# Wider column matmuls in block 0, and 64-row tile pairs for gate and up of the last 512 rows

## The chip, the cores and the metric

The kernel runs on one core of one Trainium2 chip. The metric is the device time of one execution in microseconds (us). A core has a matrix engine (TensorE, PE in the profile, with its weight loads listed apart as PEld), a vector engine (VectorE, DVE), a scalar engine (ScalarE, ACT), GpSimd (POOL) and a sync engine (SyncE, SP) whose queue issues nearly all transfers (DMAs). The engines run side by side and wait for one another by semaphores. Matmuls write to PSUM, a buffer of eight banks; this kernel uses it as four tiles of two banks each. Everything else lies in SBUF.

## The reference, cut to what matters

Input and output are 2048 rows (S) of 576 values (D), in bf16. The rows pass a modulated layer norm, a long convolution over the rows, a gate, a second modulated layer norm and a feed-forward block of width 4608 (F):

```python
mod = (silu(c) @ w_mod).reshape(1, 6, 1, 576)      # sa, ca, ga, sb, cb, gb
h = layernorm(x) * (1 + ca) + sa
x = x + ga * A(h, k, v, shift_k, ssm_k, ssm_D)     # h * (causal convolution of kv with ssm_k, + kv * D)
h = layernorm(x) * (1 + cb) + sb
gate = h @ w1                                      # 2048x576 @ 576x4608
up   = h @ w3
x = x + gb * ((silu(gate) * up) @ w2)              # 2048x4608 @ 4608x576
```

The feed-forward block has most of the arithmetic. The change touches two places: how the columns `1 + cb` and `sb` are computed from `c` and `w_mod`, and how `gate` and `up` of the last 512 rows are computed.

## The kernel before, in words

**Blocks.** The convolution works on blocks of 256 rows, numbered 0 to 7. `first_block` (lines 628 to 713) does block 0 alone. Its instructions on DVE, ACT and PE are pinned to the written order by `in_order`. The feed-forward block works on four row blocks of 512 rows, r = 0 to 3 (`row_blocks`, line 1033): for each, `stream` computes the hidden values `h3` (gate, up, SiLU and product), and then `down` multiplies them with `w2`. The steps of the convolution of the next two blocks are woven into `stream` and `down` of r = 0 to 2 by a planner: each piece of feed-forward work adds its cost in us to a due time (`advance`), and steps are emitted until the due time is spent. During r = 3 nothing is left to weave in. Outside of `first_block` the order on each engine comes from the compiler's scheduler, which keeps the written order as a priority and passes over instructions that its model has as not ready.

**The columns of block 0.** The modulation row is needed as columns for the second layer norm, since there the features lie on partitions. `mod_columns` (lines 236 to 251) computes them on PE: for each of the two vectors (`cb`, `sb`) and each of six slices j of 128 or 64 features, five matmuls over the 576 inputs (four with 128 rows and one with 64) with a slice of `w_mod` as the stationary operand and one column of `crep` as the moving one. `crep` (line 202) holds silu(c) repeated in 128 equal columns. The results lie in columns j of a PSUM bank, and ACT copies five of them to `cbcol` and `sbcol` (lines 250 and 251). After it, in order on PE, come: the 16 matmuls of 288 columns of `w_spectrum(1)` (line 299), six matmuls whose result nobody reads (`warm`, line 626), the transposes of the first 128 normalised rows (`turn_split`, line 578), and so on to the first matmuls of the feed-forward block. The transposes also need `h2row` from DVE (line 477).

**Gate and up.** `h2T` holds the normalised rows, transposed, as five slices of the 576 features: four of 128 partitions, and the last 64 features in slice 4, there twice, on partitions 0 to 63 and 64 to 127. One weight tile `wst` holds 512 hidden columns (one group fc of four columns blocks f of 128): slices 0 to 3 for gate, 5 to 8 for up, and slice 4 has the 64 remaining rows of gate on partitions 0 to 63 and those of up on 64 to 127. `load_w13` (line 861) fills it with four DMAs: 512 KB and 64 KB each for `w1` and `w3`. Two such tiles take turns in r = 3. In `stream` one item is one f: `full` (line 916) makes eight matmuls of 128 rows and 512 columns, four for gate and four for up, in two PSUM banks; `rest` (line 927) makes the two matmuls of 64 rows, which lie on different halves of the array and write different banks. For r = 3 the items go in fours: `full` of items 0 and 1, `rest` of items 0 to 3, `hide` of items 0 and 1, then `full` and `hide` of items 2 and 3. `hide` (line 931) is ACT (SiLU of gate, line 934, copy of up, line 936) and DVE (the product, line 938). The order of the SP queue in r = 3 is, for each group, the two 64 KB loads (line 868) and then the two 512 KB loads (line 867); each waits until PE has done with what lies there.

Of the kernel before, what the change touches and what calls it, by code (L numbers as in the profile page):

```python
# [9 lines left out]
BF16 = mybir.dt.bfloat16  # L10
F32 = mybir.dt.float32
I32 = mybir.dt.int32
ALU = mybir.AluOpType
ACT = mybir.ActivationFunctionType

P = 128
# [6 lines left out]
NF = F // P  # L23
RB = 512
NRB = S // RB
FC = 4
# [17 lines left out]
class _Kernel:  # L44
# [27 lines left out]
    def setup(self):  # L72
        nc, const = self.nc, self.const
        nc.scalar.preload_act_table(ACT.Silu)
        self.ident = const.tile([P, P], BF16, name="ident")
        self.npi = const.tile([P, 1], F32, name="npi")
        self.ppi = const.tile([P, 1], F32, name="ppi")
        self.neghalf = const.tile([P, 2], F32, name="neghalf")
        self.shk = const.tile([P, 4, D], BF16, name="shk")
        self.drow = const.tile([9, 64], BF16, name="drow")  # L80
        self.dcol = const.tile([P, 5], BF16, name="dcol")
        self.h3 = const.tile([P, NF, RB], BF16, name="h3")
        self.wm = self.h3[:].rearrange("p a b -> p (a b)")
        self.wst = [const.tile([P, 9, FC * P], BF16, name=f"wst{i}") for i in range(NW13)]
        self.w2m = self.wst[2]
        self.h2T = [const.tile([P, 5, RB], BF16, name=f"h2T{i}") for i in range(2)]
        self.h2row = const.tile([P, 2, 640], BF16, name="h2row")
        self.knat = const.tile([P, 5, B], BF16, name="knat")
        self.Xd = self.dram.tile([NBLK, P, 6 * D], BF16, name="Xd")
        self.Vd = self.dram.tile([NBLK, P, 6 * D], BF16, name="Vd")  # L90
        self.arow = const.tile([P, D], BF16, name="arow")
        self.brow = const.tile([P, D], BF16, name="brow")
        self.cbcol = const.tile([P, 5], F32, name="cbcol")
        self.sbcol = const.tile([P, 5], F32, name="sbcol")
        self.gbrow = const.tile([P, D], BF16, name="gbrow")

        self.Fb = const.tile([P, 5, 2, P], BF16, name="Fb")
        self.Fk = const.tile([P, 3, 2, P], BF16, name="Fk")


        self.arow_i = self.hp.tile([P, 2, P], I32, name="b_row", tag="sg")
        coli = self.small.tile([P, 4], I32, name="b_coli", tag="b_coli", bufs=1)
        self.acol = self.small.tile([P, 4], F32, name="b_col", tag="b_col", bufs=1)
        nc.gpsimd.iota(self.arow_i[:], pattern=[[2, 2], [4, P]], base=1, channel_multiplier=0)
        nc.gpsimd.iota(coli[:, 0:2], pattern=[[2, 2]], base=1, channel_multiplier=4)
        nc.gpsimd.iota(coli[:, 2:4], pattern=[[2, 2]], base=0, channel_multiplier=4)
        nc.vector.tensor_copy(self.acol[:], coli[:])
        nc.vector.memset(self.npi[:], -math.pi)
        nc.vector.memset(self.ppi[:], math.pi)
        nc.vector.memset(self.neghalf[:], -0.5)  # L110
        self.one = self.small.tile([1, P], BF16, name="one", tag="one", bufs=1)
        nc.vector.memset(self.one[:], 1.0)
        nc.vector.memset(self.dcol[:], 0.0)
        self.ang = {}
        self.angles(nc.gpsimd, 0)
        make_identity(nc, self.ident[:])
        nc.gpsimd.memset(self.knat[64:P, 4, :], 0.0)
        nc.gpsimd.memset(self.h2T[0][:, 0, :], 0.0)
# [117 lines left out]
    def mod_columns(self):  # L236

        nc = self.nc
        w5 = self.wm[:, 0:5 * 6 * D].rearrange("p (a d) -> p a d", a=5)
        ps = self.ps()  # L240
        for i, m in enumerate((4, 3)):
            for j in range(6):
                lo = min(P * j, 512)
                n = P if j < 4 else 64
                out = ps[0:n, i, j:j + 1] if j < 5 else ps[64:P, i, 4:5]
                for ct in range(5):
                    k = P if ct < 4 else 64
                    nc.tensor.matmul(out, w5[0:k, ct, m * D + lo:m * D + lo + n],
                                     self.crep[0:k, ct, 0:1], start=(ct == 0), stop=(ct == 4))
        nc.scalar.activation(self.cbcol[:], ps[:, 0, 0:5], ACT.Copy, bias=1.0)  # L250
        nc.scalar.copy(self.sbcol[:], ps[:, 1, 0:5])


    def load_kv(self, s, between=None):
# [626 lines left out]
    def stream(self, r, jobs, rate, size):  # L881
# [65 lines left out]
        for k in range(0, len(items), size):  # L947
# [11 lines left out]
            for m in late:  # L959
                full(m, False)  # L960
                hide(m)

    def down(self, r, rate):
        nc = self.nc
        for h in range(2):

            tail = r == NRB - 1 and h == 1
            accs = [self.ps() for _ in range(4 if tail else 2)]
            acc = [accs[t][:, 0, 0:H] if tail else accs[t // 2][:, t % 2, 0:H] for t in range(4)]
            for f0 in range(0, NF, W2C):  # L970
                w = _ap(self.w2m, (h * NF + f0) // W2C % NW2 * W2C * H, [[H, W2C], [1, H]])
                nc.sync.dma_start(w, self.w2[f0 * P:(f0 + W2C) * P, h * H:(h + 1) * H]
                                  .rearrange("(a p) d -> p a d", p=P))
                last = f0 + W2C == NF
                order = [(f, t) for f in range(W2C) for t in range(4)]
                if last:
                    order = [(f, t) for t in range(4) for f in range(W2C)]
                for f, t in order:
                    nc.tensor.matmul(acc[t],  # L979
                                     self.h3[:, f0 + f, t * P:(t + 1) * P], w[:, f, :],  # L980
                                     start=(f0 + f == 0), stop=(f0 + f == NF - 1))
                if h == 1 and f0 // W2C == 5 and r + 1 < NRB:

                    self.end()
                    self.turn_all(2 * r + 3)
                if (f0 // W2C) % 4 == 3:

                    leave = ((self.keep_v, 3), (self.keep_v, 2), (self.keep_x, 2), (self.keep_x, 3)) if r == 0 else ()
                    for keep, i in leave[2 * h + f0 // (4 * W2C):][0:1]:
                        keep(i)  # L990
                self.advance(rate * W2C * 4 * 0.126)
            for t in range(4):
                s, cc = 2 * r + t // 2, t % 2
                x1 = self.xo[s]
                g = self.lnp.tile([P, H], BF16, name="og", tag="og", bufs=2)
                nc.vector.tensor_mul(g[:], acc[t], self.gbrow[:, h * H:(h + 1) * H])  # L996
                nc.vector.tensor_add(x1[:, cc, h * H:(h + 1) * H], x1[:, cc, h * H:(h + 1) * H], g[:])
                if r == NRB - 1:
                    rows = self.out[B * s:B * (s + 1), h * H:(h + 1) * H].rearrange("(p c) d -> p c d", c=2)
                    nc.sync.dma_start(rows[:, cc, :], x1[:, cc, h * H:(h + 1) * H])  # L1000
                elif h == 1 and cc == 1:
                    nc.sync.dma_start(self.out[B * s:B * (s + 1), :].rearrange("(p c) d -> p c d", c=2),
                                      x1[:])
# [29 lines left out]
    def row_blocks(self, n1):  # L1033
        for r in range(NRB):
            cost = 0
            if r + 1 < NRB:
                s0 = 2 * r + 2

                self.begin(self.conv(s0), FIRST_DUE if r == 0 else 0.0)
                cost = CONV_US[r]  # L1040
            time = 110.0 * 0.85 - (N1 * 1.03 if r == 0 else 0)
            rate = cost / time
            if r == 0:

                jobs = [(fc, 256, 512, None, None) for fc in (n1 - 2, n1 - 1)]

                new = [(n1 + i, 0, RB, b, None) for i, b in enumerate((2, 1, 2))]
                again = [(fc, 256, 512, b, None) for fc, b in enumerate((0, 0, 1, 0))]
                while new or again:
                    jobs += new[0:1] + again[0:1]  # L1050
                    new, again = new[1:], again[1:]
            else:
                spills = {1: (self.keep_x, 1), 2: (self.keep_v, 0), 4: (self.keep_v, 1)} if r == 1 else {}
                jobs = [(fc, 0, RB, (r + fc) % 2, (lambda f, i: lambda: f(i))(*spills[fc]) if fc in spills else None)
                        for fc in range(NF // FC)]
            self.stream(r, jobs, rate, 4 if r == NRB - 1 else 2)
            self.down(r, rate)
            self.end()

# [52 lines left out]
```

## Time and profile before

| | |
|---|---|
| median of 5 runs | 518.87 us (518.47 to 519.67) |
| profiled execution | 517.44 us, of which 515.3 us are the span from the first to the last instruction |
| PE busy | 497.0 us (96%), 3362 matmuls |
| DVE, ACT, POOL busy | 340.9, 294.2, 55.7 us |
| mean granted clock of PE | 0.996 |
| line 248, the one-column matmuls | 60, from 22.3 to 26.0 us |
| lines 916 and 927 with r = 3 | 288 and 72 matmuls, from 404.2 to 476.1 us |
| line 979, `down` of r = 3 | 288 matmuls, from 476.1 to 511.5 us |

The busy time of an engine is the time in which at least one of its instructions is under way. Matmuls are pipelined: one of 512 columns lasts 379 ns from its start to its modelled end, but the next one starts 216 ns after it. So the pace of PE is read from start to start, not from the durations. "PEclk" is the share of its full clock that PE was granted in a stretch. The profile also follows the work that ended last back through time, step by step, to what released each piece; that is called the chain below. A "wait" names the engine and line that ended it; "issue" is idle time for which the profile shows no cause.

### The profile page before, as it was taken

The numbers are of one execution on the slowest core, as the hardware profiler recorded it, in microseconds if no ns is written. First come the engines' busy times: TensorE is split into PE (matmuls) and PEld (weight loads), VectorE is DVE, ScalarE is ACT, GpSimd is POOL, SyncE is SP. The second block draws the span as 40 slices with busy tenths as digits, with TensorE's granted clock in tenths as the row PEclk, the third lists the DMA queues.
The fourth block names the chain that finished last, engine by engine and source line by source line (L and its number), as shares of the span: only waits on it lengthen the run. The fifth ranks groups of instructions, "written<-read, shape, count | busy, mean of one in ns | idle before, by whom it ended". The sixth has DMA issues, their size and how long they took to land.

```text
span 515.3 us, 8723 instructions
## 1 busy us (share of the span) xinstructions
PE 497.0 (96%) x3362; PEld 293.7 (57%) x3362; DVE 340.9 (66%) x515; ACT 294.2 (57%) x581; POOL 55.7 (11%) x109
## 2 busy tenths in 40 slices
PE   7999989998999999999999899999999999999997
PEld 3667764556787444344787443434688544444775
DVE  8898899999993364997999984299660212112012
ACT  7668689577443569658553365976816345545000
POOL 3303003104040001203010000120101000000000
PEclk9989999999999999999999999999999999999999
DMA  8957949688979857558999763545455454450462
GB/s 278 316 157 232 296 163 295 190 259 264 297 240 340 259 176 242 172 168 281 354 344 363 269 196 121 198 148 176 141 139 142 144 175 132 153 170 6 119 180 70
DMA packets 102205, 107.77 MB, mean 209 GB/s; under 512 B 5075, under 2 KB 94228, under 8 KB 102164
## 3 DMA queue, kind: packets, MB, share of 16 engines
q1 hardware_dynamic: 102142, 107.21, 65.7%
q8 instruction: 26, 0.43, 0.3%
q14 instruction: 15, 0.12, 0.1%
q10 hardware_dynamic: 22, 0.01, 0.0%
HBM read 96.00 MB, written 11.21 MB: 208 GB/s over the span
## 4 chain that ended last, share of the span: by engine, by line
PE 65%; DVE 20%; ACT 6%; DMA 5%; issue 2%; SPq 1%; DVEq 0%; ACTq 0%
PE ps L916 36%; PE ps L979 18%; PE ps L927 5%; DVE p L410 4%; DVE z L412 3%; DMA wst<-in_B_w_dram 2%; PE ps L313 2%; DMA X<-Xd 2%; PE ps L539 1%; DVE h L938 1%; DVE z L405 1%; DVE kvt L334 1%; ACT junk L440 1%; DVE kv L335 1%; ACT sg L934 1%
## 5 line engine op out<-in xcount | busy, mean ns | idle before, releaser
L916 PE MATMUL ps<-h2T,wst 128*128 128x512 bf16 (+1 forms) x1344 | 264.9, 349 | 2.4 <-ACT h2T L601 1.6
L916 PEld LDWEIGHTS <-wst 128*128 128x128 bf16 x1344 | 127.7, 98 | 122.9 <-issue 19.8
L934 ACT ACTIVATE sg<-ps 128x512 bf16<-128x512 f32 x144 | 86.8, 603 | 112.3 <-PE ps L927 67.5
L979 PE MATMUL ps<-wst,h 128*128 128x288 bf16 x1152 | 145.5, 286 | 3.2 <-ACT u L936 2.2
L979 PEld LDWEIGHTS <-h 128*128 128x128 bf16 x1152 | 112.4, 98 | 32.9 <-issue 4.2
L938 DVE TENSOR_TENSOR h<-sg,u 128x512 bf16<-128x512 bf16 x144 | 60.7, 425 | 96.4 <-ACT u L936 96.3
L936 ACT CAST u<-ps 128x512 bf16<-128x512 f32 x144 | 84.8, 589 | 0.2 <-DVE h L938 0.2
L410 DVE TENSOR_TENSOR p<-X,V 128x3456 bf16<-128x3456 bf16 x28 | 54.8, 1958 | 5.3 <-DMA X<-Xd 5.1
L412 DVE TENSOR_TENSOR z<-z,p 128x3456 bf16<-128x3456 bf16 x28 | 54.8, 1958 | 0.2
L996 DVE TENSOR_TENSOR og<-ps,gbrow 128x288 bf16<-128x288 f32 x32 | 13.2, 453 | 48.8 <-PE ps L979 48.8
L927 PE MATMUL ps<-h2T,wst 64*128 64x512 bf16 (+1 forms) x336 | 42.4, 349 | 0.0
L440 ACT ACTIVATE junk<-x 128x576 bf16<-128x576 bf16 x54 | 37.7, 698 | 0.5
L601 ACT ACTIVATE h2T<-ps,sbcol,cbcol 128x256 bf16<-128x256 bf16 x35 | 16.8, 571 | 24.1 <-PE ps L571 24.1
L927 PEld LDWEIGHTS <-wst 64*128 64x128 bf16 x336 | 11.3, 94 | 27.2 <-issue 24.4
L455 POOL TENSOR_SCALAR l2m<-l2s 128x2 f32<-128x2 f32 x6 | 8.7, 1444 | 153.0 <-ACT junk L440 153.0
L566 ACT ACTIVATE h2row<-x,l2n,l2r 128x576 bf16<-128x576 bf16 (+1 forms) x24 | 13.8, 646 | 12.5 <-POOL l2n L460 12.5
L334 DVE TENSOR_TENSOR kvt<-kh,shk 128x1152 bf16<-128x1152 bf16 x24 | 18.1, 756 | 3.3 <-DMA kh<-in_A_k_dram 3.2
L335 DVE TENSOR_TENSOR kv<-kv,kvt 128x1152 bf16<-128x1152 bf16 x24 | 18.1, 756 | 0.3
L455 POOL TENSOR_SCALAR l1m<-l1s 128x2 f32<-128x2 f32 x7 | 3.0, 423 | 141.3 <-ACT junk L440 141.3
L315 ACT CAST X<-ps 128x576 bf16<-128x576 f32 x24 | 15.5, 657 | 0.0
L405 DVE TENSOR_TENSOR z<-X,V 128x3456 bf16<-128x3456 bf16 x7 | 13.7, 1956 | 2.3 <-DMA X<-Xd 2.3
L745 ACT CAST y<-ps 128x576 bf16<-128x576 f32 x14 | 8.4, 653 | 10.5 <-PE ps L539 10.5
(137 smaller groups left out, 362.1 us busy)
## 6 DMA issues: line engine op xcount, KB each, us to landing
wst<-in_B_w_dram SPq DMA_DIRECT2D x80, 512.0 KB, 4.7
wst<-in_B_w_dram SPq DMA_DIRECT2D x72, 288.0 KB, 3.5
X<-Xd SPq DMA_DIRECT2D x8, 864.0 KB, 5.8
Xd<-X SPq DMA_DIRECT2D x6, 864.0 KB, 5.4
wst<-in_B_w_dram SPq DMA_DIRECT2D x80, 64.0 KB, 2.9
kh<-in_A_k_dram SPq DMA_DIRECT2D x7, 720.0 KB, 8.2
Vd<-V SPq DMA_DIRECT2D x4, 864.0 KB
V<-Vd SPq DMA_DIRECT2D x4, 864.0 KB
```

Source lines behind the costliest of these rows:

```text
L334: nc.vector.tensor_mul(tmp[:], kh[:, 3 - j:5 - j, :], tap(j))
L335: nc.vector.tensor_add(kv[:], kv[:], tmp[:])
L405: nc.vector.tensor_mul(self.accs[s][:], X[:], V[:])
L410: nc.vector.tensor_mul(p[:], X[:], V[:])
L412: nc.vector.tensor_add(z[:], z[:], p[:])
L440: self.nc.scalar.activation(junk[:], src[:, i, :], func, accum_out=out[:, col:col + 1])
L916: nc.tensor.matmul(gus[k][:, i, a * n:(a + 1) * n], w[:, 5 * i + ct, (fi + a) * P:(fi + a + 1) * P], hT[:, ct, t0:t1], start=(first and ct ...
L927: nc.tensor.matmul(gus[k][:, i, a * n:(a + 1) * n], w[rows, 4, (fi + a) * P:(fi + a + 1) * P], hT[rows, 4, t0:t1], start=(first and a == 0 ...
L934: nc.scalar.activation(sg[:], gus[k][:, 0, :], ACT.Silu)
L936: nc.scalar.copy(u[:], gus[k][:, 1, :])
L938: nc.vector.tensor_mul(self.h3[:, f:f + m, t0:t1], sg[:].rearrange("p (a t) -> p a t", a=m), u[:].rearrange("p (a t) -> p a t", a=m))
L979: nc.tensor.matmul(acc[t], self.h3[:, f0 + f, t * P:(t + 1) * P], w[:, f, :], start=(f0 + f == 0), stop=(f0 + f == NF - 1))
```

## The change

In `mod_columns` each matmul takes 100 columns of `crep` in place of one, and so writes 100 equal columns; ACT then reads every hundredth. For r = 3 `stream` is replaced by `stream_halves`. There every matmul of gate and up is one of 64 rows. They come in pairs, one on partitions 0 to 63 and one on 64 to 127 of the same slice. Pass 0 of an f (`part(f, 0)`) gives gate the lower halves and up the upper halves, in five pairs, the fifth being slice 4. Pass 1 (`part(f, 1)`) swaps the two in four pairs: up gets the lower halves and gate the upper ones. So in each pair the two matmuls write different banks, and a bank is written from both halves of the array one after the other. So that pass 1 of an f does not begin before pass 0 is done, GpSimd writes one word (`tok`) after the last matmul of pass 0, and the first matmul of pass 1 waits for that word. Between pass 0 and pass 1 of f lie pass 1 of f-1 and pass 0 of f+1. The loads of the weights stand at the same place in the program, at the first f of a group.

```diff
+        self.tok = const.tile([1, 1], F32, name="tok")
...
-                out = ps[0:n, i, j:j + 1] if j < 5 else ps[64:P, i, 4:5]
+                out = ps[0:n, i, 100 * j:100 * (j + 1)] if j < 5 else ps[64:P, i, 400:500]
...
-                                     self.crep[0:k, ct, 0:1], start=(ct == 0), stop=(ct == 4))
-        nc.scalar.activation(self.cbcol[:], ps[:, 0, 0:5], ACT.Copy, bias=1.0)
-        nc.scalar.copy(self.sbcol[:], ps[:, 1, 0:5])
+                                     self.crep[0:k, ct, 0:100], start=(ct == 0), stop=(ct == 4))
+        nc.scalar.activation(self.cbcol[:], ps[:, 0, 0:500:100], ACT.Copy, bias=1.0)
+        nc.scalar.copy(self.sbcol[:], ps[:, 1, 0:500:100])
...
+    def wait_for(self, later, first):
+
+        self.tc.add_manual_dep(
+            later, first.name,
+            mybir.DependencyInfo(mybir.DependencyClass.Sync, mybir.DependencyReason.DATA),
+            reason="both halves of the rows write this bank, one after the other")
+
+    def stream_halves(self, r):
+
+        nc = self.nc
+        hT = self.h2T[r % 2]
+        newest = lambda: nc.cur_bb.bb.instructions[-1]
+        gus, ws, marks = {}, {}, {}
+
+        def part(f, swap):
+            w = ws[f // FC]
+            cols = slice(f % FC * P, (f % FC + 1) * P)
+            for ct in range(4 if swap else 5):
+                for rows, i in ((slice(0, 64), swap), (slice(64, P), 1 - swap)):
+                    nc.tensor.matmul(gus[f][:, i, :], w[rows, 5 * i + ct if ct < 4 else 4, cols], hT[rows, ct, :],
+                                     start=swap == 0 and ct == 0, stop=swap == 1 and ct == 3)
+                    if swap == 1 and ct == 0 and i == 1:
+                        self.wait_for(newest(), marks.pop(f))
+            if swap == 0:
+                first = newest()
+                nc.gpsimd.memset(self.tok[:], 0.0)
+                marks[f] = newest()
+                self.wait_for(marks[f], first)
+
+        def hide(f):
...
+        for f in range(NF + 1):
+            if f < NF:
+                if f % FC == 0:
+                    self.load_w13(f // FC, (r + f // FC) % 2)
+                    ws[f // FC] = self.w13.pop(f // FC)
+                gus[f] = self.ps()
+                part(f, 0)
+            if f > 0:
+                part(f - 1, 1)
+                hide(f - 1)
...
-            self.stream(r, jobs, rate, 4 if r == NRB - 1 else 2)
+            if r == NRB - 1:
+                self.stream_halves(r)
+            else:
+                self.stream(r, jobs, rate, 2)
```

`hide` inside `stream_halves` is the same three instructions as before, for one f.

## Prediction

> **What bounds the kernel now.** I read the page's totals and chain first: PE is busy for 497.0 of 515.3 us and has 65% of the chain, so PE time saved late in the kernel is time saved. Next comes the chain in order of time around the last row block (start, us, what):
>
> ```profile
> 398.50 5.88 PE ps L979 x48
> 404.38 3.45 PE ps L916 x16
> 407.83 0.97 PE ps L927 x8
> 408.80 7.01 PE ps L916 x32
> 415.81 0.97 PE ps L927 x8
> ...
> 471.70 0.97 PE ps L927 x8
> 472.67 3.56 PE ps L916 x16
> 476.23 33.86 PE ps L979 x276
> ```
>
> From 398 us to 510 us it is PE alone. ACT is busy for 36.8 us and DVE for 16.6 of these 71.9 us of gate and up, POOL for nothing. A group of 32 full matmuls and 8 of 64 rows takes 7.01 + 0.97 = 7.98 us. The waits of the weight loads in this stretch say what is not pure work:
>
> ```profile
> PEld L916 <- issue: 3.8, 9, 0.4
> PEld L927 <- issue: 3.8, 9, 0.4
> ```
>
> Nine times per direction the weight loads stand still for 0.4 us, at each change between 128-row and 64-row matmuls. In the timeline, start to start, full matmuls follow each other after 215.7 ns; the change to 64 rows takes 312 ns (407.452 to 407.764) and the change back 308 ns (408.425 to 408.733). In between the four pairs start at 407.764, 407.990, 408.206 and 408.422: after 226 ns for the first, then 216 ns per pair, the second of a pair 3 ns after the first. A pair so costs what one full matmul costs.
>
> For the other place I read stretches of 3.4 us (us, PE busy, granted clock, DMA share, GB/s), and the timeline:
>
> ```profile
> 22.66:26.07 3.41, 3.41 (x56) 1.00 1.02 373
> 26.07:29.49 3.42, 3.42 (x16) 0.50 1.10 328
> 29.49:32.90 3.41, 3.41 (x24) 1.00 0.71 213
> ```
> ```profile
> 22.31 3.72 PE L248 MATMUL ps<-crep,h 128*128 128x1 bf16 x60
> ...
> 29.44 0.63 DVE L477 TENSOR_SCALAR h2row<-x,l2mv,l2r 128x576 bf16<-128x576 bf16 x2
> ...
> 29.61 1.46 PE L626 MATMUL ps<-shk,ident 128*128 128x512 bf16 x6
> ...
> 30.90 0.44 PE L578 MATMUL ps<-ident,h2row 128*128 128x128 bf16 x5
> ```
>
> While the one-column matmuls run PE looks busy, but streams next to nothing: 56 columns in 3.41 us. At the end of that stretch the clock drops to half, for just one stretch, in which line 299's matmuls start every 240 ns. PE reaches the transposes at 30.90, when their input from DVE (29.44 + 0.63 = 30.07) has long been there.
>
> **What the Trainium skill says.** "TensorE: Matmul & The Clock Gate", Part 1: the clock follows activity in free-running windows of about 3.4 us and is halved after an idle one. The trace agrees: 3.413 us at 0.50. In Part 3 the same page has matmuls on different row groups run together, some 4 ns apart; here 3 ns. "TensorEngine Tiling (Array Packing)", Key Properties, says that a change of tiling mode drains the engine; the trace shows 96 and 92 ns over the usual spacing. The same page, Gotcha 1, says that different row tiles may not use one PSUM bank at the same time, which is why the change swaps banks and orders the passes; no run here shows the contrary.
>
> **The change, part by part.** *Pairs.* Before, the stage runs from 404.215 to 476.064 us: 71.85 us. Its work is 36 f of nine slots (eight full matmuls and one pair), 324 x 0.2157 = 69.89 us; the rest, 1.96 us, is nine groups with 0.217 each, which is 96 + 92 ns for the changes and some 10 ns for the first matmul after each. After, it is 36 x (5 + 4) = 324 pairs, again 69.89 us, and one change in and one out, 0.22 us: 70.11 us. Saved: 1.74 us. It adds 288 matmuls with their weight loads, four instructions per 216 ns; line 248's loads and matmuls start every 25 ns, so issuing them is covered.
>
> *The GpSimd word.* 36 memsets, and a wait on PE's first matmul of each second pass, with all of PE queued behind it, and ACT's `hide` behind PE. The trace has no such memset in this stretch. From the last start of the first pass: 379 ns to its end, about 80 ns to POOL (the usual gap between its dependent operations here), about 100 to 310 ns for a memset (the four 128x1 ones took 99 to 102 ns, line 117's 312), 40 ns back to PE (a matmul at 32.891 began 41 ns after its release): 0.6 to 0.8 us. The cover is pass 1 of f-1 and pass 0 of f+1, nine pairs or 1.94 us; for the first f only five (1.08 us), for the last only four (0.86 us). Both count from the end of a pair's 216 ns slot, so they hold too. Cost from nothing to a few tenths at the two ends; I take nothing. Without the cover it would be 0.6 to 0.8 us x 36, over 20 us.
>
> *Weight loads.* No DMA is added, but their window shrinks: a tile comes free at the end of pass 1 of its last f, which now runs after pass 0 of the next group's first f. The next use is three f later, 3 x 1.94 = 5.83 us, less 0.16 for the last matmul's end, 5.67 us (7.8 before). Both large loads are now wanted at once. Before:
>
> ```profile
> 411.53 1.26 SPq L867 DMA_DIRECT2D wst<-in_B_w_dram  x2
> ```
>
> Issued from 411.53, their last packet ended at 416.05, 4.5 us later, with the second issue 0.86 us after the first. Issued back to back they need about as long or less. With 1.1 us to spare I take nothing. The 64 KB loads come free 2.8 us earlier, with pass 0. If they stood between the large ones in the queue, they would cost some 0.5 us each, still inside.
>
> *Columns.* Line 248 sets 60 matmuls in 3.65 us: about 25 to 39 ns apart within a slice, 96 and 106 ns at the changes to and from 64 rows. At 100 columns a matmul streams for 100/512 of 213 ns, 41.7 ns, and follows after some 44. Within a slice of 128 the starts then lie 55, 44 and 44 ns apart against 39, 25 and 25, 54 ns more, and each of the two changes waits about 40 ns longer: 134 ns per slice of 128, about 107 where slices are 64 wide. 8 x 134 + 4 x 107 = 1.5 us later. The gain stands against it: if the clock holds, line 299 takes 16 x 122.5 ns (line 979's spacing for 288 columns) = 1.96 us, not 3.64. The six fillers would end, and the transposes start, at 27.47 + 1.96 + 1.29 = 30.72 in place of 30.90: 0.18 us earlier. Does the clock hold? The window would now stream for 5 x 41.7 ns in about 425, 49%. Summing the columns of the recorded matmuls, I find windows of 48% (67.0 to 70.5) and 53% (125 to 128.5) with no drop, and the one that dropped at 4%. So it most likely holds. The bounds: 1.15 us later at the transposes, if it drops at 26.07 all the same (line 248 ends at 28.15, line 299 at 30.76, fillers 32.05). Where the window lies otherwise, so that the clock of before never fell, before could start the transposes at 30.13, and after is 0.6 us later. ACT's strided copies have five columns as before; `cbcol` is wanted only at 31.33, which covers their later start.
>
> **Sum.** Against the profiled execution: 517.44 - 1.74 - 0.18 = 515.5 us. The median lies 1.43 us higher; taken from it, 518.87 - 1.92 = 516.95, so 517.0 us. The 1.74 are at the end of the chain and carry over whole. The 0.18 at 33 us may be lost on the way, since DVE and DMAs share the chain between 33 and 290 us. The scheduler also sees longer matmuls in block 0 and may shift a few instructions later on; I allow 1 us either way.
>
> **Rivals.** *The first block takes back most of it.* Either clock case: -1.74 + 1.15 = -0.6, or -1.74 + 0.6 = -1.1, some 518.1 us; with shifts from the scheduler that is no change (0.2% is 1.04 us, about the spread of the runs before, and less can't be told from nothing). For it: the window is free-running, so the drop may not be in every execution. Against: the profiled execution has it.
>
> *Pairs do not hold 216 ns over a long stretch: slower.* Place: the 324 pairs. At 5.4 ns more per pair the gain is gone, from 8.6 ns on the kernel is over 0.2% slower; at 15 ns, the distance of the next weight loads in a burst (407.760 to 407.775), it is +4.9 - 1.7 = +3.1 us, 522 us. The order of the pairs is the scheduler's: if it puts lower and upper halves apart where it believes a load to be late, an f's first pass takes 5 x 0.216 = 1.08 us more. For it: no stretch before has over four pairs. Against: three spacings in a row of 216 ns, with the loads of the third and fourth pair already made during the pair before.
>
> *Nothing gained from the tiles* because the weights come late: if the large loads took 6.7 us and not 4.5, each of seven groups would wait about 1 us, +5 us in sum, 524 us. Against: no other large transfer runs then (DMA share 0.41).
>
> **Numbers.** Forecast as above 0.62 (own range 516.0 to 517.8); first block gives back 0.22 (517.2 to 519.6); pairs or their order 0.11 and late weights 0.05, both over 520. Faster by over 0.2% comes from 0.6 of the first and a little of the second: 0.65; same 0.19; slower 0.16. The range 515.8 to 519.7 leaves out the two slow cases and a few in a hundred below.
>
> **What would show it.** Right: lines of the new matmuls start every 216 ns in pairs, from about 404 to 474 us, no "issue" waits of weight loads inside, no PE wait on POOL, clock 1.00 at 26 to 29.5 us, line 248 about 5.2 us long. Wrong: waits of PE on POOL or on DMA wst every fourth f, halves that run singly, a clock of 0.50 after line 248, or another middle part between 33 and 404 us.

## The result: slower by 0.22%

Over all runs the change takes 519.45 us against 518.28 us before, a ratio of 1.0022 (95% interval 1.0014 to 1.0029), or 1.17 us more. The forecast was 517.0 us, faster. The profiled execution takes 519.67 us, its span 517.4 us against 515.3 us. Lines have moved: line n of the kernel before is n + 1 after in the middle part, 248 is 249, 299 is 300, 405 is 406. The new pairs are line 983, their words line 989, and `down` is line 1026.

The chain around the last row block (start, us, what):

```profile
401.42 5.88 PE ps L1026 x48
407.30 32.76 PE ps L983 x303
440.06 5.78 DMA wst<-in_B_w_dram
445.84 0.05 issue
445.88 32.12 PE ps L983 x296
478.00 33.96 PE ps L1026 x276
```

It is one stretch of pairs now, but for one transfer of weights in the middle. The stage starts 3 us later than before (407.23, before 404.22) and runs to 477.93: 70.70 us, before 71.85. So it gives 1.15 us back, and what these two executions lose lies ahead of it. The waits of this stretch:

```profile
POOL tok L989 <- PE ps L983: 77.1, 36, 12.3
...
PEld L983 <- DMA wst<-in_B_w_dram: 1.3, 2, 1.0
PE ps L983 <- DMA wst<-in_B_w_dram: 0.5, 1, 0.5
...
PEld L983 <- issue: 0.2, 1, 0.2
```

POOL waits for PE, as it should; no wait of PE on POOL is listed. The nine stops per direction at changes between 128 and 64 rows are gone. From start to start the pairs keep 216 ns all through; the longest exception is 869 ns at 445.0.

In block 0, the same three stretches (us, PE busy, clock, DMA share, GB/s) and PE's timeline:

```profile
22.66:26.07 3.41, 3.41 (x44) 1.00 1.02 360
26.07:29.49 3.42, 3.42 (x35) 1.00 1.10 340
29.49:32.90 3.41, 3.41 (x26) 1.00 0.83 236
```
```profile
22.71 5.31 PE L249 MATMUL ps<-crep,h 128*128 128x100 bf16 x60
27.96 2.13 PE L300 MATMUL ps<-kT,Fk 128*128 128x288 bf16 x16
...
31.22 0.44 PE L579 MATMUL ps<-ident,h2row 128*128 128x128 bf16 x5
```

The clock holds. From the first column matmul to the first transpose PE takes 8.51 us (22.71 to 31.22), before 8.59 (22.31 to 30.90). The forecast was 0.18 us earlier; it is 0.08, and this is not where the time went either.

Where it went is seen on DVE, some ten microseconds later. Before:

```profile
39.85 0.76 DVE L335 TENSOR_TENSOR kv<-kv,kvt 128x1152 bf16<-128x1152 bf16 x1
40.52 0.42 DVE L938 TENSOR_TENSOR h<-sg,u 128x512 bf16<-128x512 bf16 x1
40.85 0.75 DVE L337 TENSOR_TENSOR kv<-kv,vt 128x1152 bf16<-128x1152 bf16 x1
41.52 1.95 DVE L405 TENSOR_TENSOR z<-X,V 128x3456 bf16<-128x3456 bf16 x1
```

After:

```profile
39.99 1.96 DVE L406 TENSOR_TENSOR z<-X,V 128x3456 bf16<-128x3456 bf16 x1
41.86 0.43 DVE L939 TENSOR_TENSOR h<-sg,u 128x512 bf16<-128x512 bf16 x1
42.19 0.76 DVE L336 TENSOR_TENSOR kv<-kv,kvt 128x1152 bf16<-128x1152 bf16 x1
42.93 0.42 DVE L939 TENSOR_TENSOR h<-sg,u 128x512 bf16<-128x512 bf16 x1
43.28 0.75 DVE L338 TENSOR_TENSOR kv<-kv,vt 128x1152 bf16<-128x1152 bf16 x1
```

The order has changed: the long product z of block 1 now stands ahead of the last two steps of `kv`. PE needs `kv` for the spectrum of block 1; it does not need z yet. PE's first matmuls of that spectrum, before and then after:

```profile
41.76 2.12 PE L299 MATMUL ps<-kv,Fb 128*128 128x288 bf16 x16
```
```profile
44.17 1.02 PE L300 MATMUL ps<-kv,Fb 128*128 128x288 bf16 x7 [2.10 <-DVE kv L338]
```

Before, PE comes to them with no wait noted; after, it stands idle for 2.10 us until line 338 is done. Counted from the first matmul of gate and up (32.89 and 33.20), the spectrum starts after 8.86 us before and after 10.97 us now. The programs show the same: outside the new stage, SP's order is the same in both, POOL differs by the 36 words and PE by the width of 60 matmuls, but DVE's order differs in a few places between its 70th and its 90th instruction, and ACT's in one swap. How far the delay is carried on can be read from the first matmul of gate and up to the first one of the last row block. In the three profiled kernels with z ahead of the end of `kv` (the change and two of the experiments below) this takes 373.83 to 375.45 us; in the nine others 371.32 to 373.49 us.

### The profile page after: what moved, and what is told of

Its sections match the earlier page's. It is cut to its first block, busy times and chain, and to the rows that moved or that the text cites. A ratio compares the mean times of both kernels' runs of the same rounds, so it can differ in the third digit from the quotient of the medians.

```text
span 517.4 us, 9370 instructions
## 1 busy us (share of the span) xinstructions
PE 496.7 (96%) x3650; PEld 294.5 (57%) x3650; DVE 341.1 (66%) x515; ACT 293.9 (57%) x581; POOL 59.6 (12%) x145
## 4 chain that ended last, share of the span: by engine, by line
PE 69%; DVE 16%; ACT 6%; DMA 4%; issue 2%; POOL 1%; SPq 1%; POOLq 0%; ACTq 0%; DVEq 0%
PE ps L917 26%; PE ps L1026 19%; PE ps L983 13%; PE ps L928 4%; DVE p L411 4%; DMA wst<-in_B_w_dram 4%; DVE z L413 3%; ACT junk L441 2%; PE ps L314 2%; PE ps L540 2%; PE ps L300 1%; PE ps L220 1%; DVE h L939 1%; DVE kvt L335 1%; DVE kv L336 1%
## 5 line engine op out<-in xcount | busy, mean ns | idle before, releaser
L917 PE MATMUL ps<-h2T,wst 128*128 128x512 bf16 (+1 forms) x1056 | 201.0, 341 | 2.3 <-ACT h2T L602 1.6
L917 PEld LDWEIGHTS <-wst 128*128 128x128 bf16 x1056 | 100.2, 98 | 87.3 <-issue 15.5
L939 DVE TENSOR_TENSOR h<-sg,u 128x512 bf16<-128x512 bf16 x108 | 45.4, 424 | 39.3 <-ACT u L937 39.2
L983 PE MATMUL ps<-h2T,wst 64*128 64x512 bf16 x648 | 70.3, 376 | 0.5 <-DMA wst<-in_B_w_dram 0.5
L983 PEld LDWEIGHTS <-wst 64*128 64x128 bf16 x648 | 31.3, 94 | 39.2 <-DMA wst<-in_B_w_dram 1.3
L928 PE MATMUL ps<-h2T,wst 64*128 64x512 bf16 (+1 forms) x264 | 33.3, 342 | 0.9 <-ACT X L316 0.9
L456 POOL TENSOR_SCALAR l1m<-l1s 128x2 f32<-128x2 f32 x7 | 5.6, 806 | 141.7 <-ACT junk L441 141.7
L928 PEld LDWEIGHTS <-wst 64*128 64x128 bf16 x264 | 8.6, 94 | 22.4 <-issue 21.6
```

The costliest lines, as they stand in the source:

```text
L917: nc.tensor.matmul(gus[k][:, i, a * n:(a + 1) * n], w[:, 5 * i + ct, (fi + a) * P:(fi + a + 1) * P], hT[:, ct, t0:t1], start=(first and ct ...
L928: nc.tensor.matmul(gus[k][:, i, a * n:(a + 1) * n], w[rows, 4, (fi + a) * P:(fi + a + 1) * P], hT[rows, 4, t0:t1], start=(first and a == 0 ...
L939: nc.vector.tensor_mul(self.h3[:, f:f + m, t0:t1], sg[:].rearrange("p (a t) -> p a t", a=m), u[:].rearrange("p (a t) -> p a t", a=m))
L983: nc.tensor.matmul(gus[f][:, i, :], w[rows, 5 * i + ct if ct < 4 else 4, cols], hT[rows, ct, :], start=swap == 0 and ct == 0, stop=swap == ...
```

## Experiments

Theory O: the order on DVE costs. Theory W: the work of the longer matmuls costs. Theory H: the pairs of half tiles are slow. All ratios are to the kernel before, with runs on the same chip, 95% interval in brackets.

**100 columns alone.**

```diff
-                out = ps[0:n, i, j:j + 1] if j < 5 else ps[64:P, i, 4:5]
+                out = ps[0:n, i, 100 * j:100 * j + 100] if j < 5 else ps[64:P, i, 400:500]
...
-                                     self.crep[0:k, ct, 0:1], start=(ct == 0), stop=(ct == 4))
+                                     self.crep[0:k, ct, 0:100], start=(ct == 0), stop=(ct == 4))
...
```

> The 100-column matmuls alone, the last row block as before. Theory O (order): with 100 columns the compiler's scheduler orders DVE differently after block 0, the 1.96 us product z at line 405 ahead of the last steps of kv, and that is what costs: 2.3 to 2.9 us slower than before, with line 299's matmuls of x_spectrum(1) starting about 2.4 us later. Theory W (work): the longer matmuls themselves cost, 1.6 us at most where the clock would have held anyway, less otherwise: 0 to 1.6 us slower. Theory H (halves): the tile pairs are what is slow, and this kernel is within 0.5 us of before.

520.01 us, 1.0031 (1.0017 to 1.0044): 1.4 us slower by the medians. The spectrum starts 10.96 us after the first matmul of gate and up, again behind a wait for `kv`:

```profile
43.62 1.79 PE L299 MATMUL ps<-kv,Fb 128*128 128x288 bf16 x7 [2.09 <-DVE kv L337]
```

In this execution PE was busy for only 1.33 of the 3.42 us around the wait, and the clock was 0.50 in the next 3.41 us, a second cost (us, PE busy, clock, DMA share, GB/s). The profiled execution of the change does not have that.

```profile
40.29:43.71 3.42, 1.33 (x13) 1.00 0.97 279
43.71:47.12 3.41, 3.41 (x16) 0.50 0.96 293
```

H is out as the cause of the loss. O expected more than this, W's upper end fits the time, so it takes the next ones to tell.

**The pairs alone.** One column, and the new stage. Of the change's edit this much stays, with the new functions:

```diff
-            self.stream(r, jobs, rate, 4 if r == NRB - 1 else 2)
+            if r == NRB - 1:
+                self.stream_halves(r)
+            else:
+                self.stream(r, jobs, rate, 2)
```

> The 64-row pairs alone, block 0 with one column as before, so DVE's order outside the last row block is that of before. O and W: 1.1 to 1.7 us faster than before (the stage of gate and up in 70.1 to 70.8 us in place of 71.85). H: no faster, or slower by 1 us, with the stage as long as before or longer.

518.05 us, 0.9991 (0.9975 to 1.0008): half a microsecond faster by the medians, and not told from no change. The stage takes 70.56 us, inside what was expected. The 1.3 us that it saves would be 0.9975, at the edge of the interval, so whether they all arrive is not told; the last experiment has a part of the answer.

**Both parts with 80 columns.** At 80 the order on DVE is that of before.

```diff
-                out = ps[0:n, i, 100 * j:100 * (j + 1)] if j < 5 else ps[64:P, i, 400:500]
+                out = ps[0:n, i, 100 * j:100 * j + 80] if j < 5 else ps[64:P, i, 400:480]
...
-                                     self.crep[0:k, ct, 0:100], start=(ct == 0), stop=(ct == 4))
+                                     self.crep[0:k, ct, 0:80], start=(ct == 0), stop=(ct == 4))
```

> Both parts, with 80 columns in place of 100. At 80 the DVE order is that of before. O: 1.0 to 1.9 us faster than before. W: 80% of the cost of 100 columns stays, so about 0.3 us slower to 0.5 us faster than before. H: 1 us slower.

517.70 us, 0.9992 (0.9969 to 1.0015). The interval is too wide to decide between O and W by itself.

**Both parts with 100 columns, z held behind kv.** Only the order on DVE differs from the change.

```diff
         nc.vector.tensor_mul(kv[:], kv[:], vt[:])
+        self.kv_last = nc.cur_bb.bb.instructions[-1]
...
-        yield from self.pair(self.X[0], self.V[1], 1)
+        first = self.pair(self.X[0], self.V[1], 1)
+        with self.tc.issue_after(self.kv_last):
+            c = next(first)
+        yield c
+        yield from first
```

> Both parts with 100 columns, and the product z of block 1 (line 405) made to issue after the last step of kv on DVE. DVE's order is then that of before but for two V steps. O: 1.0 to 1.9 us faster than before, about 2.5 us faster than the change. W: like the change, about 1.2 us slower than before. H: the same, 1 us slower.

517.79 us, 0.9980 (0.9964 to 0.9997), faster than before where the change is slower. W expected 1.2 us slower and falls. The spectrum of block 1 no longer waits:

```profile
41.64 2.12 PE L300 MATMUL ps<-kv,Fb 128*128 128x288 bf16 x16
```

It starts 8.81 us after the first matmul of gate and up. Of all kernels run this is the only one whose interval lies below 1, and only just; the same kernel with its instructions moved, below, has 0.9988 (0.9968 to 1.0008). Neither loses; that the pinned change is faster is not certain.

**The order alone.** The kernel before, one column, no pairs; z written ahead of the last step of `kv` (in the change it stands ahead of the last two).

```diff
-        yield from self.kv_rows(1)
+        rows = self.kv_rows(1)
+        for _ in range(3):
+            yield next(rows)
         yield from self.v_block(1)
         yield from self.pair(self.X[0], self.V[1], 1)
+        yield from rows
```

> The kernel before with one column and without tile pairs; only DVE's order is that of the change: the product z of block 1 issues ahead of the last multiply of kv. O (order): 1.3 to 2.4 us slower than before, line 299's matmuls of x_spectrum(1) starting 1.5 to 2.5 us later. W (the longer matmuls are the cost): no difference, within 0.4 us of before.

520.15 us, 1.0035 (1.0018 to 1.0053), 1.3 us slower by the medians, without one longer matmul. DVE and PE show the same picture as with the change:

```profile
40.95 1.95 DVE L405 TENSOR_TENSOR z<-X,V 128x3456 bf16<-128x3456 bf16 x1
42.82 0.41 DVE L941 TENSOR_TENSOR h<-sg,u 128x512 bf16<-128x512 bf16 x1
43.16 0.75 DVE L337 TENSOR_TENSOR kv<-kv,vt 128x1152 bf16<-128x1152 bf16 x1
```
```profile
44.05 1.14 PE L299 MATMUL ps<-kv,Fb 128*128 128x288 bf16 x8 [2.17 <-DVE kv L337]
```

**80 columns alone.** The matmuls of the third experiment in the kernel before.

> 80 columns alone, with DVE's order of before. O: between 0.3 us faster and 0.7 us slower than before, since what PE spends longer (about 1.2 us) is taken from fillers and from the wait for DVE. W: about 1.3 us slower, four fifths of what 100 columns alone cost.

518.05 us, 0.9987 (0.9970 to 1.0004), by the medians 0.8 us faster, a little more than O expected. The 60 matmuls take 4.59 us from first to last start (3.54 with one column, 5.08 with 100), and no loss follows. W falls here too.

**100 columns alone, z held behind kv.** The edits of the first and the fourth experiment together. O expected to be within 0.6 us of before, W 1.4 us slower.

> 100 columns alone, with the product z of block 1 issued after the last step of kv; no tile pairs. O (order): within 0.6 us of before, so 1.3 to 2.3 us faster than 100 columns with the scheduler's own order; line 299's matmuls of x_spectrum(1) start 8.8 us after the first matmul of gate and up, as before, not 11.0. W (work of the longer matmuls): 1.4 us slower than before, like 100 columns alone.

518.13 us, 0.9999 (0.9985 to 1.0014). The first matmul of gate and up starts at 32.65 us, the spectrum 8.81 us after it and without a wait:

```profile
41.47 2.12 PE L299 MATMUL ps<-kv,Fb 128*128 128x288 bf16 x16
```

The same 60 matmuls cost 0.31% or nothing, according to DVE's order. O is shown from both sides: the order without the columns costs, the columns without the order don't. Why the scheduler's order tips between 80 and 100 columns no run shows.

**Is the slow issue of a load due to instructions being fetched?** Theory F: a load of weights that is issued slowly meets a fetch of instructions, and moving the instructions frees it. In the change, SP's timeline has such a load:

```profile
436.79 1.11 SPq L869 DMA_DIRECT2D wst<-in_B_w_dram  x2
439.59 2.20 SPq L868 DMA_DIRECT2D wst<-in_B_w_dram  x2
444.56 1.12 SPq L869 DMA_DIRECT2D wst<-in_B_w_dram  x2
448.03 0.93 SPq L868 DMA_DIRECT2D wst<-in_B_w_dram  x2
```

The pair of large loads takes 2.20 us to issue at 439.59 and 0.93 at 448.03. The second one began to issue at 440.06, and among the DMA packets the same moment has one of 16 KB on the queue that fetches instructions (1.31 us long). PE then waits 0.65 us beyond its usual spacing. The pairs alone, both parts with 80 columns, and the held version have the slow issue at the same load too (1.28 to 1.42 us), with 0.3, 0 and 0.7 us of PE's time. So the held version and the pairs alone were run again with PE's instructions moved on by 56, in place of four fillers that nobody reads:

```diff
-        self.warm(6, busy)
+        self.warm(2, busy, 32)
...
+        for _ in range(narrow):
+            self.nc.tensor.matmul(ps[:, 0, 0:1], self.ident[:], src[:, 0:1], start=True, stop=True)
```

> Both parts with 100 columns and DVE's order of before, and four of the six unread fillers of block 0 (512 columns each) are made 32 fillers of one column, so that PE's instruction stream is 56 instructions ahead in the last row block. Theory F (fetch): the one slow issue on the SP queue there (1.3 to 1.7 us in place of 0.46) comes from meeting a 16 KB fetch of instructions at the same time; moved by about 3 us it is gone, no matmul waits for weights, and the stage of gate and up takes 70.1 us; 1.7 us faster than before. Against F: the slow issue stays at the same load, with a stall of 0.5 to 0.7 us, stage 70.7.

> The tile pairs alone with one column, with the same 32 short fillers. F: stage of gate and up in 70.1 us, 1.7 us faster than before. Against F: 70.7 us and 0.5 to 1.1 us faster. Set against the kernel with 100 columns and the same order, it says what the columns themselves are worth: nothing to 0.6 us in favour of one column.

In the first of them, the same load:

```profile
436.10 1.11 SPq L876 DMA_DIRECT2D wst<-in_B_w_dram  x2
438.90 0.92 SPq L875 DMA_DIRECT2D wst<-in_B_w_dram  x2
```

The slow issue is gone and the stages take 70.24 and 70.15 us, which speaks for F. The times do not follow: 518.08 us, 0.9988 (0.9968 to 1.0008), and 518.64 us, 0.9997 (0.9982 to 1.0013), not the 1.7 us that were expected. The second is no clean test: its narrow fillers came on top of the one-column matmuls, the clock was 0.50 for 6.83 us from 25.19, and gate and up began 11.51 us after the first column matmul.

The held version with moved instructions has other slow issues instead, of 2.0 and 1.8 us at 252 and 256 us, where the change has none over 0.8. The second of them meets a 16 KB fetch, the first meets none. In the change's own last row block two more fetches, at 413.07 and 428.32, overlap issues of small loads that take their usual 0.47 and 0.48 us. Counted over all twelve traces, after the first 30 us: of 215 issues that overlap a 16 KB fetch 35 take over 1 us, of 3266 that overlap none 42 do; of 24 that begin within 0.1 us of the start of a fetch 14 do. So slow issues are much more frequent beside a fetch, most of all at its start, but a fetch is neither enough nor needed. F stays likely for the one place, and what it is worth in the whole kernel is open.

**The words alone.** Theory T: the words make the end of the program longer. Every kernel with pairs takes 39.5 us from the first matmul of the last `down` to the end of the program; those without take 39.2. The kernel before, with 36 words that no matmul waits for:

```diff
+            if r == NRB - 1:
+                newest = nc.cur_bb.bb.instructions[-1]
+                nc.gpsimd.memset(self.tok[:], 0.0)
+                self.tc.add_manual_dep(
+                    nc.cur_bb.bb.instructions[-1], newest.name,
+                    mybir.DependencyInfo(mybir.DependencyClass.Sync, mybir.DependencyReason.DATA),
+                    reason="word")
```

> The kernel before with the 36 GpSimd words of the last row block and nothing else; no matmul waits for them. Theory T (tail): the 0.3 us more between the first matmul of the last down and the end of the program, which every kernel with tile pairs shows (39.5 us against 39.2), comes from the words: 39.5 us here, 0.3 us slower than before. Rival (tail of the pairs): it comes from the change of the array's mode on entering down: 39.2 us here, and no difference.

The tail is 39.50 us, and the kernel takes 519.69 us, 1.0017 (1.0001 to 1.0034). T holds for the tail. Its rival, that the change from 64 to 128 rows on entering `down` makes it longer, falls, since this kernel enters `down` from 128 rows. The whole time agrees with 0.3 us, but its interval is too wide to measure that. In the profiles the 0.3 us are the very last step: POOL's last instruction starts 0.37 us after the one before it, without words 0.07 us; why, no run shows. A word itself takes 88 ns, as its group in this kernel shows (busy us, mean ns of one, then the idle time before and what ended it):

```profile
L936 POOL MEMSET tok<- 1x1 f32 x36 | 3.2, 88 | 79.9 <-PE ps L928 50.5 <-PE ps L917 22.2 <-DVE h L946 7.3
```

## Why the prediction was wrong, by its own steps

**Sum.** By the profiles the change gives up 2.11 us to DVE's order (10.97 - 8.86), gains 1.15 us in the stage (71.85 - 70.70) and loses 0.29 us at the end: +1.25 us, where the medians differ by 1.17. That these two agree so well is luck in part, since the profiled spans differ by 2.16 us. The rest is 0.40 us ahead of the first column matmul, where no instruction has another order or width, 0.09 us gained from there to gate and up, and 0.60 us between the spectrum and the last row block. That last stretch alone runs from 362.46 us (the kernel before) to 364.63 us over the twelve profiles. By whole times the order costs 1.3 us (alone, by the medians) to 2.2 us (the change against the held version, by the ratios 1.0022 and 0.9980).

**The step that failed** is the sentence that the scheduler "may shift a few instructions later on; I allow 1 us either way". It put at nothing, with a margin for chance, what one mechanism makes 2.11 us in the profile. At 100 columns the scheduler puts a 1.96 us product ahead of the steps that PE waits for; at 80 it doesn't. The place could be seen before: in the trace of the kernel before, DVE's last step of `kv` and z stand right behind each other at 41 us, and PE's spectrum, at 41.76, starts 0.16 us after that step ends. DVE was at that time the engine to look at, and the prediction asked only how much later PE comes out of block 0. That the order would tip at 100 columns could not be read from that trace, but from the order of the program after. The first rival, that block 0 takes most of the gain back, looked near the right place for the wrong mechanism, and ended at "no change"; neither slow rival happened. It is luck that 519.45 us lies within the stated 515.8 to 519.7 us: the term that brought it there was put at nothing. The baseline was off as well: 518.87 us was the median of 5 runs, 518.28 is that of 79.

**Pairs.** The pace was right: 216 ns per pair over 648 matmuls, one change in and one out. The stage was sized at 70.11 us and measured at 70.08 (80 columns) to 70.75 us (held version); the difference is the late weights. The cover of the word was right: no wait of PE on POOL. That the words cost nothing was wrong by 0.3 us, at the end of the program, where nothing hides it.

**Weight loads.** "With 1.1 us to spare I take nothing" took the 4.5 us of one pair of large loads for all. In the change the pair issued from 439.59 landed only at 445.84, 6.25 us later, with one issue of 1.74 us in it, and that reached PE, 0.65 us once. The mechanism of the rival of late weights exists, but at a tenth of its price.

**Columns.** The 60 matmuls were forecast 1.5 us longer and are 1.54 longer (5.08 against 3.54 from first to last start), with starts 54, 44 and 44 ns apart within a slice as worked out. (The 213 ns for 512 columns in that sum follow from two spacings of the trace: (215.7 - 122.5) / (512 - 288) is 0.416 ns per column.) The clock holds; the window over them streamed for 59%, forecast 49%. The gain of 0.18 us at the transposes measured 0.08. The doubt about the baseline was justified: in the pairs alone, with one column, the windows lay otherwise and no drop came,

```profile
21.83:25.24 3.41, 3.41 (x51) 1.00 1.11 332
25.24:28.66 3.42, 3.42 (x47) 1.00 1.04 365
```

and its first matmul of gate and up started 9.26 us after the first column matmul, before 10.58, held version 10.49. In the words alone, with one column too, the drop lasted twice as long and that distance was 11.67 us:

```profile
24.71:28.12 3.41, 3.41 (x33) 0.50 1.08 354
28.12:31.54 3.42, 3.20 (x13) 0.50 0.99 299
```

So the wider matmuls spare a drop that does not come in every execution. Against these distances they gain up to 1.2 us or lose up to 1.2; the loss, for which the prediction had 0.6, is an estimate, since in the pairs alone the columns began 1.3 us later than before (23.59) and DVE, not PE, had the chain there. With 100 columns the distance is 10.43 to 10.49 us in all five profiles. Over many runs no difference is seen (0.9987 with 80 columns, 0.9999 with 100).

The prediction had one window that dropped, at 4%, and two that did not, at 48 and 53%. The twelve profiles narrow this down. Take windows of 3.41 us in line with the recorded drops, from 10 to 505 us, and estimate the streaming by 0.416 ns per column: the ten windows at full clock that a drop followed streamed for 4 to 34% of their time, and no other window at full clock streamed for less than 40%. A few matmuls are missing from some traces.

**What stays open** is how much of the stage's gain arrives. The held version has 0.9980 against 0.9999 for the same columns without pairs: about 1 us. The pairs alone have 0.9991 (0.9975 to 1.0008). But with 80 columns the kernel with pairs has 0.9992 and the one without 0.9987, so there nothing is gained, though its stage is the shortest of all. Less 0.3 for the end, 0.8 to 1.5 us would be expected, and the intervals hold that, but they hold zero too. The slow issues elsewhere may take a part.

## What to carry to other kernels

Where a scheduler orders the instructions, a longer instruction early in the program changes more than its own time: compare the order of every engine before and after, and look at engines that the edit does not touch. Where an engine is shared between work that somebody waits for and work that nobody waits for yet, pin the order there; here one dependency took the same change from 1.0022 to 0.9980 (0.9964 to 0.9997). Count an edit that makes a buffer's window smaller with the slowest issue of a load that the trace shows anywhere, not with the usual one: the kernel before has one of 1.38 us at 245.78, where its last row block has 0.37 to 0.60. And take the result of one profiled execution with care where differences of 1 us count.

## What was not expected of the hardware

In the kernel before, 36 words written by GpSimd in the last row block made the end 0.3 us longer (39.50 against 39.23 us), though each took 88 ns and no engine waited for it. The issue of a DMA from the SP queue, in the last row block usually 0.37 to 0.60 us, took 1.3 to 1.7 us at the same load in four kernels, at the start of a 16 KB fetch of instructions, and was back to normal when PE's instructions were moved by 56. One-column matmuls, with PE busy throughout by the profile, were followed by a granted clock of 0.50 for 3.4 us in the kernel before and for 6.8 us in the words alone, and by none in the pairs alone, while 80 and 100 columns in the same place had none in any of seven profiles. By the estimate above, the line lay between 34 and 40% of a window streamed. In the 100 columns alone a wait of 2.1 us for DVE was enough to fall under it, with 33%.
